# Immediate operands for the exponentials of a fused attention, Fourier and feed-forward kernel, with the scales of q and k chosen to cancel

## The chip, the cores and the metric

The kernel runs on one core of a Trainium2 chip. Its time is the device time of one launch in microseconds, the median of several executions. A core has five engines that run side by side and meet at semaphores: TensorE (PE in the profile, with its weight loads as PEld), VectorE (DVE), ScalarE (ACT), GpSimd (POOL) and SyncE (SP, which issues most DMAs). Each engine takes its own instructions strictly in the order in which the program gives them.

## What is computed

Attention over 8 batches of 8 heads, 576 positions and 64 columns, with a block-causal mask in blocks of 64; then on the joined heads a two-dimensional Fourier transform, whose real part is added, a layer norm and a feed-forward layer. All inputs and outputs are fp32. Cut to what matters here:

```python
scores = (1.0 / np.sqrt(D)) * np.matmul(q, k.transpose(0, 1, 3, 2))      # D = 64: 0.125
scores = np.where(mask, scores, -1000000000.0)
scores = scores - np.max(scores, axis=-1, keepdims=True)
attn = np.exp(scores)
attn = attn / (np.sum(attn, axis=-1, keepdims=True) + 1e-09)
x = np.matmul(attn, v)                                                   # heads joined: (8, 576, 512)
u = x + np.real(np.fft.fft(np.fft.fft(x, axis=1), axis=2))
un = (u - mu) / np.sqrt(var + 1e-06)
out = u + np.maximum(un @ w_ch1, 0.0) @ w_ch2
```

## The kernel before

**Precision by halves.** Matmuls run on pairs of f16 numbers, a high part and the rest, so that three matmuls stand for one in fp32. To split a tensor well, it is first multiplied by a power of two that is worked out on the chip from its sum of squares.

**Heads.** The 64 heads are numbered through. Heads 0 to 7 use q and k as fp32r numbers without such a scale (`lead`, `rest`, lines 421 to 438). Heads 8 to 63 come in pairs g = 4 to 31: `load_pair` brings q and k of two heads, `sum_qk` (line 380) squares them on ACT with a running sum, `scale` (line 461) turns the sums of v, q and k into three powers of two, `high` (line 389) writes the scaled f16 high parts on ACT, `low` (line 396) the rests on DVE, and `high_copies` and `low_copies` send them by DMA into the operands X1 and X0 of the score matmuls.

**scale.** A matmul with ones sums the three columns over the partitions. DVE copies the result to `n2` and works on the bits as integers: the exponent is halved and subtracted from a constant, for all three columns at once (two instructions). Two more instructions, on one column each, hold the scale of q back to a bound and write into column 9 of the tile `vacc` the power of two that undoes both scales and multiplies by 0.125. That column is `exps[g]`.

**One head.** `max_part` (line 576) computes the scores' row maxima in four pieces: matmuls into a PSUM bank, then TENSOR_REDUCE on DVE into the tile `M`. `shift` (line 605) transposes `M` on PE, writes the negative on ACT into `mt`, and a DMA puts it into a row of X1, so that the score matmuls subtract the maximum. `scores` (line 634) makes four pieces per head, two of 288 columns and two of 512: matmuls into a bank, then on ACT the exponential twice, once as f16 (`ph`, line 652) and once as fp32 (`p32`, named `p` in the profile, line 655), then on POOL their difference (`pl`, line 657). `p32` has two buffers, and the bank comes free when both exponentials have read it. `values` (line 663) multiplies by v with the three matmuls per block and on DVE divides by the row sums, which one column of ones in v gives. The exponentials carry a factor of 32 (2 to the PSHIFT), which the division takes out again: heads 0 to 7 get it in the shift row (line 618), heads 8 to 63 as the exponential's bias, a [128, 1] tile `lift` that holds 5 ln 2.

```python
how = {"scale": 0.125} if h < H else {"scale": exps[h // 2], "bias": lift}      # line 637, H = 8
```

**The rest.** `fourier_steps` runs the transform of each batch once its eight heads are done, `normalized_steps` the norm, and `feed_steps` the feed-forward layer, whose matmuls (into `h` and `acc`) are fed to PE between the others. In the first 220 us DVE also unpacks the two weight matrices (`weight_single`, line 1101).

**What sets the order.** The program's order on each engine is written out by a planner that runs when the program is built (lines 286 to 361 and 1205 to 1263). Work comes in steps of a dozen lanes, each with the steps that it follows, a place (about the number of the head) and a chain of costs: "D0.7" is 0.7 us on DVE, A is ACT, G and P POOL, X DVE with the port that it shares with POOL, Q the DMA queue of SP, B marks where a PSUM bank comes free. The planner books these on model queues, picks the next step that is ready, and emits its instructions by their planned start. An exponential of width w is planned with 0.19 + 0.00082 w us on ACT (`_a`, line 51), a `scale` step with 0.11 on PE, 0.2 and, after the bank, 0.7 on DVE (line 569).

Of the kernel before, what the change touches and what calls it, by code (L numbers as in the profile page):

```python
# [9 lines left out]
F32 = mybir.dt.float32  # L10
F32R = mybir.dt.float32r
F16 = mybir.dt.float16
I32 = mybir.dt.int32
AF = mybir.ActivationFunctionType
ALU = mybir.AluOpType
# [4 lines left out]
B, H, S, D = 8, 8, 576, 64  # L20
DM = H * D
FF = 4 * DM
P = 128
# [19 lines left out]
PSHIFT = 5  # L43
# [158 lines left out]
def tile_attn_fourier_ffn(  # L202
# [4 lines left out]
    const = pool("const")  # L207
# [5 lines left out]
    def ps_tile():  # L213
        return ps[current].tile([P, 512], F32, name=current)

    def mm(*args, **kw):
        return tc.keep_in_program_order(nc.tensor.matmul(*args, **kw))  # L217

    def tp(*args, **kw):
        return tc.keep_in_program_order(nc.tensor.transpose(*args, **kw))  # L220

    vector, scalar, gpsimd, sync = (Ordered(tc, x) for x in (nc.vector, nc.scalar, nc.gpsimd, nc.sync))
# [7 lines left out]
    vector.memset(ones, 1.0)  # L230
    mhalf = const.tile([P, 1], F32, name="mhalf")
    vector.memset(mhalf, -0.5)
    lift = const.tile([P, 1], F32, name="lift")
    vector.memset(lift, float(PSHIFT * np.log(2.0)))
    dft = const.tile([P, c_dft.shape[1]], F32R, name="dft")
    o = [0]

# [39 lines left out]
    for at in range(0, NCOS, P):  # L277
        w = min(P, NCOS - at)
# [17 lines left out]
    def may(step):  # L296
        return all(x in done for x in step.after) and all(x in done for x in step.need)

    def ready(step):
        r = max((done[x] for x in step.after), default=0.0)  # L300
        return max(r, min(rings[x][0] for x in lent)) if step.bank else r
# [138 lines left out]
    def load_v(g):  # L440
        V = vraw[g] = work.tile([P, 5, 2, D], F32, name="V", bufs=1)
        sync.dma_start(V.rearrange("p c h d -> p (c h d)"), v[g])
        yield
# [11 lines left out]
    def sum_v(g):  # L455
        acc = sums(g)
        junk = work.tile([P, DM], F32, name="tmp", bufs=2).bitcast(F16)[:, 0:5 * 2 * D]
        scalar.activation(junk, vraw[g].rearrange("p c h d -> p (c h d)"), AF.Square, accum_out=acc[:, 0:1])
        yield

    def scale(g):

        acc = vsums.pop(g)
        t = ps_tile()
        mm(t[:, 0:3], ones, acc[:, 0:3], start=True, stop=True)
        yield
        n2, sc = acc[:, 3:6], acc[:, 6:9]
        x = work.tile([P, 4], I32, name="pw", bufs=2)
        vector.tensor_copy(n2, t[:, 0:3])
        c = 190 + 14  # L470
        vector.tensor_scalar(
            x[:, 0:3], n2.bitcast(I32), 0x7F000000, 1, op0=ALU.bitwise_and, op1=ALU.logical_shift_right
        )
        vector.tensor_scalar(sc.bitcast(I32), x[:, 0:3], -1, c << 23, op0=ALU.mult, op1=ALU.add)
        sq, xk, e = acc[:, 7:8].bitcast(I32), x[:, 2:3], acc[:, 9:10].bitcast(I32)
        vector.scalar_tensor_tensor(sq, xk, (2 * 127 + 20 - c) << 23, sq, op0=ALU.add, op1=ALU.min)
        vector.scalar_tensor_tensor(e, xk, (3 * 127 - 3 - c) << 23, sq, op0=ALU.add, op1=ALU.subtract)
        scales[g] = sc
        exps[g] = acc[:, 9:10]
        yield  # L480

    exps = {}

    def parts_v(g):

        sc = scales[g][:, 0:1]
        V = vraw.pop(g)
        vh, vl = VH[g % 2], VL[g % 2]
        scalar.activation(vh[:, :, :, 0:D], V, AF.Copy, scale=sc)
        yield  # L490
        vector.scalar_tensor_tensor(vl, V, sc, vh[:, :, :, 0:D], op0=ALU.mult, op1=ALU.subtract)
        pairs[g] = sc
        yield

    def split_v(g):

        acc = vsums.pop(g)
        V = vraw.pop(g)
        t = ps_tile()
        mm(t[:, 0:1], ones, acc[:, 0:1], start=True, stop=True)  # L500
        yield
        sc = acc[:, 2:3]
        x = work.tile([P, 1], I32, name="pw", bufs=2)
        vector.tensor_copy(acc[:, 1:2], t[:, 0:1])
        vector.tensor_scalar(
            x, acc[:, 1:2].bitcast(I32), 0x7F000000, 1, op0=ALU.bitwise_and, op1=ALU.logical_shift_right
        )
        vector.tensor_scalar(sc.bitcast(I32), x, -1, (190 + 14) << 23, op0=ALU.mult, op1=ALU.add)
        vh, vl = VH[g % 2], VL[g % 2]
        yield  # L510
        scalar.activation(vh[:, :, :, 0:D], V, AF.Copy, scale=sc)
        yield
        vector.scalar_tensor_tensor(vl, V, sc, vh[:, :, :, 0:D], op0=ALU.mult, op1=ALU.subtract)
        pairs[g] = sc
        yield
# [39 lines left out]
    def v_lane():  # L555
        for g in range(B * H // 2):
            yield Step(
                lambda: load_v(g), 0.0, ("Q0.6", "M1.1", "L2.0"), (("N", g - 1),) if g else (), ("LV", g), place=2 * g - 2.2,
            )
            yield Step(lambda: sum_v(g), 0.0, ("t1", "A0.95", "t"), (("LV", g),) + ((("V", 2 * g - 3, 4),) if 1 < g < H // 2 else (("V", 2 * g - 5, 4),) if g > 3 else ()), ("NS", g),  # L560
                       place=2 * g - (0.6 if g < H // 2 else 1.6))
            if g < H // 2:
                yield Step(
                    lambda: split_v(g), 0.11, ("D0.46", "B", "A0.83", "X0.88"), (("NS", g),), ("N", g), True,
                    need=(("V", 2 * g - 3, 4),) if g > 1 else (), place=2 * g - 0.4,
                )
                continue
            yield Step(
                lambda: scale(g), 0.11, ("D0.2", "B", "D0.7"), (("NS", g), ("QS", g)), ("SC", g), True, place=2 * g - 1.4,
            )  # L570
            yield Step(
                lambda: parts_v(g), 0.0, ("A0.83", "X0.88"), (("SC", g),), ("N", g),
                need=(("V", 2 * g - 3, 4),), place=2 * g - 0.4,
            )
# [30 lines left out]
    def shift(h):  # L605

        t = ps_tile()
        tp(t[0:5, 0:P], M[h % 2][:, 0:5], ident)
        yield
        if h >= H:  # L610
            mt = work.tile([5, P], F32, name="mt", bufs=2).bitcast(F16)[:, 0:P]
            scalar.activation(mt, t[0:5, 0:P], AF.Copy, scale=-(2.0 ** -15))
            yield
            sync.dma_start(X1[h % NB][KM:KS, 0:640].rearrange("r (j p) -> r j p", j=5), mt)
            yield
            return
        mt = work.tile([5, P], F32R, name="mt", bufs=2)
        scalar.activation(mt, t[0:5, 0:P], AF.Copy, bias=float(8.0 * PSHIFT * np.log(2.0)), scale=-1.0)
        yield
        dst = LEAD[h % NB][KM:KS, 0:640].rearrange("r (j p) -> r j p", j=5)  # L620
        sync.dma_start(dst.bitcast(F32), mt.bitcast(F32))
        yield
# [11 lines left out]
    def scores(h, n):  # L634

        x0, x1 = (REST[h % NB], LEAD[h % NB][0:KS]) if h < H else (X0[h % NB], X1[h % NB])
        how = {"scale": 0.125} if h < H else {"scale": exps[h // 2], "bias": lift}
        i, at, chunks = PIECES[n]
        if at == 0:
            width = S if i == 0 else 512  # L640
            probs[h, i] = [work.tile([P, width], F16, name=f"p{x}{i}", bufs=1) for x in "hl"]
        ph, pl = probs[h, i]
        t = ps_tile()
        w = 0
        for c, lo, width in chunks:
            first, last = P * c + lo, P * c + lo + width
            keys = S + (P * c if c < 4 else S - P)
            mm(t[:, w:w + width], x0[:, keys:keys + P], x0[:, first:last], start=(w == 0), stop=False, skip_group_check=True)
            keys, w = keys + 64, w + width
            mm(t[:, w - width:w], x1[:, keys:keys + P], x1[:, 64 + first:64 + last], start=False, stop=True, skip_group_check=True)  # L650
        yield
        scalar.activation(ph[:, at:at + w], t[:, 0:w], AF.Exp, **how)
        yield
        p32 = work.tile([P, 512], F32, name="p32", bufs=2)
        scalar.activation(p32[:, 0:w], t[:, 0:w], AF.Exp, **how)
        yield
        gpsimd.tensor_tensor(pl[:, at:at + w], p32[:, 0:w], ph[:, at:at + w], op=ALU.subtract)
        yield
# [550 lines left out]
    while True:  # L1209
# [13 lines left out]
        for w, side in enumerate(sides):  # L1223
# [3 lines left out]
            at = max(now, ready(side))  # L1227
# [5 lines left out]
        else:  # L1233
            w = None
# [5 lines left out]
        if soon:  # L1240
            i = min(soon, key=lambda i: heads[i].place)
        elif feed and ready(filler) <= now or feed and not able:
            i = None
        elif able:
            i = min(able, key=lambda i: ready(heads[i]))
        elif any(sides):
            w = min((w for w, x in enumerate(sides) if x is not None and may(x)), key=lambda w: ready(sides[w]))
# [62 lines left out]
```

## Time and profile before

| | |
|---|---|
| median of 3 runs | 1267.94 us (1265.29 to 1270.67) |
| the profiled execution | 1268.88 us, its span 1267.1 us |
| TensorE's granted clock, mean | 0.940 |
| busy: PE, PEld, DVE, ACT, POOL | 91%, 66%, 56%, 50%, 35% of the span |

A profile is of one execution. The span runs from the first to the last instruction; an engine's busy time is the time covered by its instructions, and a busy PE is not a PE at its peak. Groups of instructions are told by the engine, the operation and the tiles, written `out<-in`; all instructions here have a helper's line (195, 217 or 220), so the tiles identify them: `ph<-ps,lift,vacc` is the first exponential of a head from 8 on, with its pointers to bias and scale, `ph<-ps` the same of heads 0 to 7. After each group stand the busy time, the mean length of one in ns, and the idle time of the engine before it with what ended that. The chain of work that ended last is followed back from the last instruction, at each step to what released it.

### The profile page before, as it was taken

How to read it: one execution, taken by the hardware profiler on the slowest of the kernel's cores; microseconds unless marked ns; L12 is line 12 of the kernel's file. 1: busy time of each engine (PE TensorE's matmuls, PEld its weight loads, DVE VectorE, ACT ScalarE, POOL GpSimd, SP SyncE). 2: the span in 40 equal slices, each digit the busy share in tenths (PEclk: the TensorE clock that was granted, in tenths of full speed). 3: DMA queues.
4: the chain of work that ended last, by engine and by line, in shares of the span. 5: the costliest groups of instructions: out<-in, count | busy, mean ns of one | idle time of the engine just before them, and what ended most of it. 6: DMA issues, size and time to landing. Idle time of an engine off the chain costs nothing.

```text
span 1267.1 us, 25203 instructions
## 1 busy us (share of the span) xinstructions
PE 1150.4 (91%) x10068; PEld 831.3 (66%) x10068; DVE 711.4 (56%) x1493; ACT 637.3 (50%) x1249; POOL 439.2 (35%) x537
## 2 busy tenths in 40 slices
PE   5772588979899999999999989999999999999998
PEld 4661366557677776677767767677777667766665
DVE  7778797755655575766657555477534424421211
ACT  5556667945666567566656457656652112111110
POOL 5656632433534433444333423425341300300000
PEclk9555787989999999999999989999999999999999
DMA  7675253342224234234233222513320110000000
GB/s 211 195 253 171 71 171 97 97 116 72 84 73 127 62 84 109 73 93 121 63 97 114 72 85 77 154 36 93 73 72 7 36 33 4 22 18 1 18 18 17
DMA packets 64939, 107.34 MB, mean 85 GB/s; under 512 B 9408, under 2 KB 35192, under 8 KB 64822
## 3 DMA queue, kind: packets, MB, share of 16 engines
q1 hardware_dynamic: 57718, 81.42, 23.1%
q10 hardware_dynamic: 4384, 16.78, 3.9%
q0 software_dynamic: 2720, 7.54, 2.1%
q8 instruction: 79, 1.29, 0.4%
q14 instruction: 38, 0.31, 0.1%
HBM read 58.52 MB, written 18.87 MB: 61 GB/s over the span
## 4 chain that ended last, share of the span: by engine, by line
PE 75%; DVE 12%; ACT 4%; DMA 3%; POOL 3%; issue 3%; SPq 0%; DVEq 0%; ACTq 0%; POOLq 0%
PE h L217 27%; PE acc L217 27%; PE ps L217 14%; PE av L217 5%; DVE W L195 3%; DVE M L195 2%; DMA lead<-mt 2%; PE ps L220 1%; ACT ph L195 1%; ACT p L195 1%; DVE tmp L195 1%; POOL pl L195 1%; DVE vacc L195 1%; DVE VL L195 1%; DMA xd<-x 1%
## 5 line engine op out<-in xcount | busy, mean ns | idle before, releaser
L217 PE MATMUL h<-uh,W 128*128 128x256 f16 x2304 | 430.5, 274 | 1.1 <-DVE ul L195 0.6
L195 POOL TENSOR_TENSOR pl<-p,ph 128x512 f16<-128x512 f32 (+1 forms) x256 | 254.6, 1000 | 408.9 <-ACT p L195 382.6
L217 PEld LDWEIGHTS <-W 128*128 128x128 f16 x3456 | 334.3, 98 | 65.9 <-issue 2.8
L217 PE MATMUL acc<-W,gh 128*128 128x512 f16 x1104 | 330.1, 380 | 0.0
L217 PE MATMUL h<-ul,W 128*128 128x256 f16 x1152 | 315.3, 274 | 0.0
L195 ACT ACTIVATE gh<-h 128x512 f16<-128x512 f32 x138 | 82.2, 596 | 269.4 <-PE h L217 269.3
L217 PE MATMUL acc<-W,gl 128*128 128x512 f16 x552 | 209.8, 380 | 0.1
L195 DVE SCALAR_TENSOR_TENSOR gl<-h,gh 128x512 f16<-128x512 f32 x138 | 94.9, 688 | 204.5 <-ACT gh L195 204.2
L195 DVE TENSOR_REDUCE M<-ps 128x1 f32<-128x192 f32 (+3 forms) x289 | 129.9, 486 | 124.4 <-PE ps L217 124.2
L195 ACT ACTIVATE ph<-ps,lift,vacc 128x288 f16<-128x288 f32 x220 | 150.8, 686 | 90.5 <-PE ps L217 90.1
L217 PE MATMUL ps<-lead 72*128 72x64 f16 (+13 forms) x693 | 160.8, 296 | 20.1 <-ACT lead L195 6.7
L217 PEld LDWEIGHTS <-gh 128*128 128x128 f16 x1104 | 104.0, 99 | 81.1 <-issue 2.3
L195 ACT ACTIVATE p<-ps,lift,vacc 128x288 f32<-128x288 f32 x220 | 150.6, 686 | 10.3 <-POOL pl L195 10.3
L217 PEld LDWEIGHTS <-ph 128*128 128x128 f16 x1920 | 115.7, 104 | 27.8 <-issue 4.7
L217 PE MATMUL av<-VH,pl 128*128 128x65 f16 x960 | 117.1, 201 | 17.6 <-POOL pl L195 16.7
L217 PE MATMUL av<-VH,ph 128*128 128x65 f16 x960 | 118.7, 203 | 2.1 <-DVE x L195 2.1
L217 PE MATMUL av<-VL,ph 128*128 128x64 f16 x960 | 118.2, 201 | 0.0
L217 PEld LDWEIGHTS <-pl 128*128 128x128 f16 x960 | 94.3, 103 | 20.6 <-POOL pl L195 19.3
L217 PE MATMUL ps<-rest 128*128 128x288 f16 (+2 forms) x348 | 96.8, 292 | 6.9 <-ACT p L195 2.9
L217 PEld LDWEIGHTS <-gl 128*128 128x128 f16 x552 | 53.9, 98 | 67.1 <-DVE gl L195 1.6
L217 PEld LDWEIGHTS <-lead 72*128 72x128 f16 (+1 forms) x672 | 58.2, 100 | 58.8 <-issue 13.1
L217 PEld LDWEIGHTS <-rest 128*128 128x128 f16 x336 | 33.4, 99 | 19.7 <-issue 2.8
(193 smaller groups left out, 1441.2 us busy)
## 6 DMA issues: line engine op xcount, KB each, us to landing
raw<-in_qk_dram SPq DMA_DIRECT2D x28, 576.0 KB
W<-in_moe_w_ch_dram ACTq DMA_DIRECT2D x14, 1024.0 KB
rest<-lead SPq DMA_DIRECT2D x72, 144.0 KB
V<-in_v_dram SPq DMA_DIRECT2D x32, 320.0 KB
xd<-x SPq DMA_DIRECT2D x32, 256.0 KB
out_dram<-u SPq DMA_DIRECT2D x32, 256.0 KB
rest<-rest SPq DMA_DIRECT2D x56, 144.0 KB
u<-xd SPq DMA_DIRECT2D x8, 512.0 KB
```

The lines of the kernel that those rows point to most:

```text
L195: x = f(*args, **kw)
L217: return tc.keep_in_program_order(nc.tensor.matmul(*args, **kw))
L220: return tc.keep_in_program_order(nc.tensor.transpose(*args, **kw))
```

## The change

It picks the scales of q and k so that their product is one: the exponent of each is a quarter of the exponent of the other's sum of squares minus a quarter of that of its own, both cut to a multiple of four. The scores then need no scale but 0.125, so the exponentials of all heads take the immediate 0.125 and no bias. The factor of 32 goes for all heads into the row that `shift` writes. The scale of v is made as before, in two instructions of its own. `exps`, `lift` and its memset go away. The planner's price for the second part of `scale` on DVE is 0.8 instead of 0.7.

```diff
-    lift = const.tile([P, 1], F32, name="lift")
-    vector.memset(lift, float(PSHIFT * np.log(2.0)))
...
         vector.tensor_copy(n2, t[:, 0:3])
-        c = 190 + 14
+        bits, to = n2.bitcast(I32), sc.bitcast(I32)
         vector.tensor_scalar(
-            x[:, 0:3], n2.bitcast(I32), 0x7F000000, 1, op0=ALU.bitwise_and, op1=ALU.logical_shift_right
+            x[:, 1:3], bits[:, 1:3], 0x7E000000, 2, op0=ALU.bitwise_and, op1=ALU.logical_shift_right
         )
-        vector.tensor_scalar(sc.bitcast(I32), x[:, 0:3], -1, c << 23, op0=ALU.mult, op1=ALU.add)
-        sq, xk, e = acc[:, 7:8].bitcast(I32), x[:, 2:3], acc[:, 9:10].bitcast(I32)
-        vector.scalar_tensor_tensor(sq, xk, (2 * 127 + 20 - c) << 23, sq, op0=ALU.add, op1=ALU.min)
-        vector.scalar_tensor_tensor(e, xk, (3 * 127 - 3 - c) << 23, sq, op0=ALU.add, op1=ALU.subtract)
+        for i in (1, 2):
+            vector.scalar_tensor_tensor(
+                to[:, i:i + 1], x[:, 3 - i:4 - i], 127 << 23, x[:, i:i + 1], op0=ALU.add, op1=ALU.subtract
+            )
+        vector.tensor_scalar(
+            x[:, 0:1], bits[:, 0:1], 0x7F000000, 1, op0=ALU.bitwise_and, op1=ALU.logical_shift_right
+        )
+        vector.tensor_scalar(to[:, 0:1], x[:, 0:1], -1, (190 + 14) << 23, op0=ALU.mult, op1=ALU.add)
         scales[g] = sc
-        exps[g] = acc[:, 9:10]
...
-                lambda: scale(g), 0.11, ("D0.2", "B", "D0.7"), (("NS", g), ("QS", g)), ("SC", g), True, place=2 * g - 1.4,
+                lambda: scale(g), 0.11, ("D0.2", "B", "D0.8"), (("NS", g), ("QS", g)), ("SC", g), True, place=2 * g - 1.4,
...
-            scalar.activation(mt, t[0:5, 0:P], AF.Copy, scale=-(2.0 ** -15))
+            c = 2.0 ** -15
+            scalar.activation(mt, t[0:5, 0:P], AF.Copy, bias=float(8.0 * PSHIFT * np.log(2.0)) * c, scale=-c)
...
-        how = {"scale": 0.125} if h < H else {"scale": exps[h // 2], "bias": lift}
...
-        scalar.activation(ph[:, at:at + w], t[:, 0:w], AF.Exp, **how)
+        scalar.activation(ph[:, at:at + w], t[:, 0:w], AF.Exp, scale=0.125)
...
-        scalar.activation(p32[:, 0:w], t[:, 0:w], AF.Exp, **how)
+        scalar.activation(p32[:, 0:w], t[:, 0:w], AF.Exp, scale=0.125)
```

More of the change, by code (lines that the diff above doesn't have):

```diff
@@ L469, in scale @@
         vector.tensor_copy(n2, t[:, 0:3])
-        c = 190 + 14
+        bits, to = n2.bitcast(I32), sc.bitcast(I32)
         vector.tensor_scalar(
-            x[:, 0:3], n2.bitcast(I32), 0x7F000000, 1, op0=ALU.bitwise_and, op1=ALU.logical_shift_right
+            x[:, 1:3], bits[:, 1:3], 0x7E000000, 2, op0=ALU.bitwise_and, op1=ALU.logical_shift_right
         )
-        vector.tensor_scalar(sc.bitcast(I32), x[:, 0:3], -1, c << 23, op0=ALU.mult, op1=ALU.add)
-        sq, xk, e = acc[:, 7:8].bitcast(I32), x[:, 2:3], acc[:, 9:10].bitcast(I32)
-        vector.scalar_tensor_tensor(sq, xk, (2 * 127 + 20 - c) << 23, sq, op0=ALU.add, op1=ALU.min)
-        vector.scalar_tensor_tensor(e, xk, (3 * 127 - 3 - c) << 23, sq, op0=ALU.add, op1=ALU.subtract)
+        for i in (1, 2):
[6 more added lines that the diff above has]
+        vector.tensor_scalar(to[:, 0:1], x[:, 0:1], -1, (190 + 14) << 23, op0=ALU.mult, op1=ALU.add)
         scales[g] = sc
-        exps[g] = acc[:, 9:10]
         yield
-    exps = {}
     def parts_v(g):
```

## The prediction

> **What bounds the kernel now.** The page comes first: span, engine shares, and the chain of work that ended last.
>
> ```profile
> span 1267.1 us, 25203 instructions
> PE 1150.4 (91%) x10068; PEld 831.3 (66%) x10068; DVE 711.4 (56%) x1493; ACT 637.3 (50%) x1249; POOL 439.2 (35%) x537
> PE 75%; DVE 12%; ACT 4%; DMA 3%; POOL 3%; issue 3%; SPq 0%; DVEq 0%; ACTq 0%; POOLq 0%
> PE h L217 27%; PE acc L217 27%; PE ps L217 14%; PE av L217 5%; DVE W L195 3%; DVE M L195 2%; DMA lead<-mt 2%; PE ps L220 1%; ACT ph L195 1%; ACT p L195 1%; DVE tmp L195 1%; POOL pl L195 1%; DVE vacc L195 1%; DVE VL L195 1%; DMA xd<-x 1%
> ```
>
> PE carries the time. ACT, which the change relieves, is busy for half of the span and holds 4% of the chain. An average over stages says little, so the next view cuts the span into stretches: the exponentials that the change touches (heads 8 and up) lie between 147 and 946 us, as a later table shows. The columns are window, length, then busy time of PE, PEld, DVE, ACT and POOL, the granted clock, the DMA share and GB/s.
>
> ```profile
> 147.00:350.00 203.00, 169.40 (x1594) 121.98 (x1595) 142.55 (x302) 134.76 (x267) 81.41 (x101) 0.89 0.37 104
> 350.00:500.00 150.00, 148.39 (x1444) 107.20 (x1442) 91.36 (x215) 91.77 (x180) 57.43 (x69) 1.00 0.33 88
> 500.00:946.00 446.00, 431.47 (x4219) 313.08 (x4217) 271.17 (x604) 271.61 (x530) 179.79 (x217) 0.99 0.31 86
> 946.00:1267.00 321.00, 316.28 (x2205) 218.14 (x2202) 95.74 (x173) 52.18 (x100) 34.75 (x59) 1.00 0.07 21
> ```
>
> PE idles 203 - 169.4 = 33.6 us in the first stretch, 1.6 in the second, 14.5 in the third: 49.7 us altogether is what any relief of the other engines could win between 147 and 946 us. Whose idle time it is, the waits of PE in that window say (total, times, longest):
>
> ```profile
> PE av L217 <- POOL pl L195: 14.8, 13, 5.9
> PE ps L217 <- ACT p L195: 10.2, 9, 2.4
> PE ps L217 <- DVE M L195: 7.5, 7, 1.6
> PE acc L217 <- DVE M L195: 6.6, 1, 6.6
> ```
>
> The first two are the tail of the exponential path: scores on PE, `ph` and `p` on ACT, `pl` on POOL, values on PE; and a bank of scores comes free when `p` has been read. The last two are row maxima queued on DVE, with no exponential in them.
>
> **The exponentials.** The change turns the two per-partition operands of line 652 and 655 (scale from `vacc`, bias from `lift`) into immediates, for heads 8 to 63. Heads 0 to 7 already run this very call, so the trace holds both forms. First the grouped rows (busy, mean ns), then the window table restricted to the tile `lift` (DVE, then ACT):
>
> ```profile
> L195 ACT ACTIVATE ph<-ps,lift,vacc 128x512 f16<-128x512 f32 x110 | 86.0, 783 | 17.6 <-PE ps L217 17.2
> L195 ACT ACTIVATE ph<-ps,lift,vacc 128x288 f16<-128x288 f32 x110 | 64.9, 590 | 73.0 <-PE ps L217 72.9
> L195 ACT ACTIVATE ph<-ps 128x288 f16<-128x288 f32 x8 | 3.2, 402 | 0.5 <-PE ps L217 0.5
> L195 ACT ACTIVATE ph<-ps 128x512 f16<-128x512 f32 x5 | 3.0, 606 | 1.8 <-PE ps L217 1.8
> 147.00:350.00 203.00, 0.00 (x0) 68.62 (x112) 0.89 0.37 104
> 350.00:946.00 596.00, 0.00 (x0) 204.81 (x336) 0.99 0.32 87
> ```
>
> There are 112 + 336 = 448 such instructions (56 heads, 4 pieces, 2 outputs). One is shorter by 590 - 402 = 188 ns at 288 columns and by 783 - 606 = 177 ns at 512. Neighbours on ACT overlap, though, so the price of one is the distance between starts, read from the timeline:
>
> ```profile
> 604.98 0.58 ACT L195 ACTIVATE p<-ps,lift,vacc 128x288 f32<-128x288 f32 x1
> 605.45 0.59 ACT L195 ACTIVATE ph<-ps,lift,vacc 128x288 f16<-128x288 f32 x1
> 606.40 0.79 ACT L195 ACTIVATE ph<-ps,lift,vacc 128x512 f16<-128x512 f32 x1
> 607.07 0.80 ACT L195 ACTIVATE p<-ps,lift,vacc 128x512 f32<-128x512 f32 x1
> 63.85 0.40 ACT L195 ACTIVATE ph<-ps 128x288 f16<-128x288 f32 x1
> 64.14 0.40 ACT L195 ACTIVATE p<-ps 128x288 f32<-128x288 f32 x1
> 67.14 0.60 ACT L195 ACTIVATE ph<-h 128x512 f16<-128x512 f32 x1
> 67.64 0.59 ACT L195 ACTIVATE p<-h 128x512 f32<-128x512 f32 x1
> ```
>
> With pointers 0.47 and 0.67 us from start to start, with immediates 0.29 and 0.50: the overlap doesn't eat the saving, each instruction gives back 0.17 to 0.18 us, and I take 0.18. ACT gets 448 x 0.18 = 81 us back, but ACT is idle half of the time, so what counts is the part on the path. The chain that ended last, cut to the two stretches, gives that part:
>
> ```profile
> by line: PE h L217 19.7%; PE ps L217 14.0%; PE acc L217 12.5%; DVE W L195 7.6%; DVE M L195 6.1%; PE av L217 5.8%; issue 5.3%; DVE vacc L195 2.5%; ACT p L195 1.9%; POOL pl L195 1.8%; POOL ag L195 1.7%; ACT ph L195 1.6%; POOL u L195 1.5%; PE
> by line: PE acc L217 27.6%; PE h L217 25.7%; PE ps L217 19.8%; PE av L217 8.4%; issue 2.4%; PE ps L220 1.8%; DMA lead<-mt 1.8%; ACT ph L195 1.8%; ACT p L195 1.5%; DVE tmp L195 1.2%; DVE M L195 0.7%; DVE gl L195 0.6%; POOL pl L195 0.6%; DVE
> ```
>
> From 147 to 350 us, `ph` and `p` hold 3.5% of 203 = 7.1 us; from 350 to 946 us 3.3% of 596 = 19.7 us; together 26.8 us. Equal counts of both widths make a mean distance of 0.57 us, of which 0.18 goes, 32%: **-8.5 us**. The bounds: nothing, if PE is late anyway wherever the chain runs through ACT (in the second stretch PE idles only 1.6 us); and all the waits of PE on `p` and `pl`, 10.2 + 14.8, less the single one of 5.9 that ACT doesn't cause: there POOL has its indirect loads in front of `pl`, the last of them the row below. That leaves 19.1 us.
>
> ```profile
> 265.05 0.89 POOL L195 DMA_INDIRECT U<-xd,rows  x1 [0.30 <-issue]
> ```
>
> **The longer scale step.** `scale` issued five DVE instructions per pair of heads (a copy, two on three columns, two on one) and now issues six: the copy, one on two columns, two on one, two more on one for v. That is one more, for 28 pairs. The rows of its present parts:
>
> ```profile
> L195 DVE SCALAR_TENSOR_TENSOR vacc<-pw,vacc 128x1 int32<-128x1 int32 x56 | 14.7, 263 | 1.9
> L195 DVE TENSOR_SCALAR vacc<-pw 128x3 int32<-128x3 int32 x28 | 7.4, 264 | 1.0
> L195 DVE TENSOR_SCALAR pw<-vacc 128x3 int32<-128x3 int32 x28 | 6.6, 236 | 1.0
> ```
>
> One more is 0.25 us, 28 of them 7 us of DVE's time. Queued behind it on DVE stand the next row maxima, whose lateness PE shows above. On the chain `vacc` on DVE holds 2.5% of 203 = 5.1 us; a call puts 2 x 0.263 + 0.264 = 0.79 us there under this name, so some 6.4 calls lie on it, and 6.4 x 0.25 = **+1.6 us**. In 350 to 946 us the name is not among those shown, so it is under 0.6% of 596 = 3.6 us, at most 4.6 calls and 1.1 us. Hence 0 to 2.7 us; I take 1.5, near the row that is there. The scale of q and k is written by the fourth instruction as before, so ACT's `high` copies wait no longer; that of v is now last instead of third, which its step hides, being placed a full head later; without that cover it is two instructions, 0.5 us, in each of those calls.
>
> **Edits with one answer.** The shift now carries the constant as an immediate on a Copy. Both forms are in the trace, without it (f16) and with it (fp32r, heads 0 to 7), and cost the same:
>
> ```profile
> L195 ACT ACTIVATE mt<-ps 5x128 f16<-5x128 f32 x54 | 13.9, 257 | 37.9 <-PE ps L220 37.7
> L195 ACT ACTIVATE mt<-ps 5x128 fp32r<-5x128 f32 x2 | 0.5, 258 | 2.4 <-PE ps L220 2.4
> ```
>
> The memset of `lift` lies at the start beside the first loads: nothing. No DMA, matmul or wait is added or moved in the text; but the planner's price of `scale` on DVE goes from 0.7 to 0.8, which can reorder steps (rival three).
>
> **The clock.** Around 335 us the exponential path holds PE up, and the granted clock falls just after (windows; then PE's waits in 330 to 341 us):
>
> ```profile
> 330.00:340.00 10.00, 5.40 (x61) 3.67 (x59) 7.99 (x18) 8.69 (x17) 5.62 (x8) 1.00 0.36 105
> 340.00:350.00 10.00, 9.55 (x95) 8.31 (x96) 5.58 (x12) 7.61 (x15) 3.30 (x4) 0.83 0.56 159
> PE ps L217 <- ACT p L195: 2.3, 2, 1.3
> PE av L217 <- POOL pl L195: 2.1, 2, 1.1
> PE ps L220 <- DVE M L195: 0.7, 1, 0.7
> ```
>
> A clock of 0.83 over 10 us costs 1.7 us. If those waits shrink far enough the dip goes; I can't tell, and take half, **-0.9 us**. The Trainium skill (TensorE: Matmul & The Clock Gate, HAM oscillation) has it that the clock holds as long as PE has no gap over about 3.4 us; by that rule gaps of 1.3 us cost no clock, and the sum would be -7.0 instead of -7.9. The row speaks against the rule: no wait here is over 1.3 us and the clock went down.
>
> **Sum:** -8.5 + 1.5 - 0.9 = -7.9 us. The profiled execution took 1268.88 us (span 1267.1 and 1.8 around it), 0.9 above the median of 1267.94; taken off the median: **1260.0 us**. A change of 0.5%, 6.3 us, is about what can be told from none.
>
> **Rivals.** *One, PE is the bound and the freed time stays on ACT.* For it: from 350 to 946 us PE is busy 579.9 of 596 us, and three quarters of the chain time counted above lies there. Against it: the waits on `p` and `pl` by name. It gives 0 to -5 us, 1263 to 1268, and up to 1270 with the DVE instruction on the path. A second reading leads there too: measured by weight loads, PE is as full before 946 us as after, 542.3 of 799 us against 218.1 of 321, 68% in both, and after 946 us there are no exponentials to wait for. The Trainium skill (Trainium Kernel Development and Optimization, Performance Expectations) holds load share, not matmul busy time, to be the good measure; by it nothing is to be won and the time stays at 1268. I weigh it low, since the matmuls of the two stretches differ (65-column values matmuls load as often for fewer columns), and the idle gaps are measured directly. Chance 0.21, of it 0.05 for this reading.
>
> *Two, the waits close altogether.* The plan's own prices for an exponential, 0.43 and 0.61 us (line 51's formula), lie below the measured distance now and above it afterwards, so ACT would run to plan; -19.1 + 1.5 - 1.7 = -19.3, 1248.6 us. Against it: where ACT runs without a break, as in 330 to 340 us, six exponentials give 1.1 us where PE waits 4.4. Chance 0.15 for a gain over 12 us.
>
> *Three, the new plan costs more.* Place: the first 220 us, where DVE unpacks the weights while the first paired heads are scaled. The extra 0.1 us in DVE's booked time can put a weight unpacking ahead of a row maximum. Price: PE's one wait of 6.6 us on such a maximum, with a dip of the clock like that above (1.7), 8.3 us. One of them cancels the gain (1268.3); from two on it is slower, 1276.6 us. For it: from 147 to 350 us DVE is the fullest engine but PE, and W on DVE holds 7.6% of the chain. Against: each booking moves by a tenth of a microsecond only, and reordering can as well remove such a wait. Chance 0.09.
>
> That the immediates don't shorten the instruction is ruled out by the rows of heads 0 to 7, and has no chance of its own.
>
> **Numbers.** Forecast (a gain of 5 to 12 us) 0.55, of which 0.12 is under 6.3 us. Faster: 0.43 + 0.15 = 0.58; within 0.5%: 0.12 + 0.21 = 0.33; slower 0.09. The range goes from rival two with no cost on DVE, 1267.9 - 19.1 - 1.7 = 1247, to rival one with the instruction's cost and no gain, 1270; rival three and the edges are left out.
>
> **What would show it.** Right: the exponentials at 402 and 606 ns in all heads, ACT's busy time down by some 80 us, `p` and `pl` waits of PE in 147 to 946 us down by about a third to a half, `ph` and `p` on the chain near 18 us, DVE busy up by 7 us, the stretch after 946 us as long as now. Wrong: durations unchanged; PE's waits moved to row maxima or a DMA with the same total; or new gaps of several microseconds before 220 us.

## The result, and the profile after

The changed kernel takes 1254.01 us (median of 4, 1252.18 to 1254.87) against 1268.18 us before (median of 4): a ratio of 0.9887, 95% interval 0.9863 to 0.9911, or 14.2 us less. The forecast was 1260.0 us, 7.9 less, so the direction and the range held. The experiments below show that its reason did not: nearly all of the gain comes from another order of the same work, and none that could be measured from the shorter exponentials.

The page of the changed kernel, its span, engine shares and chain:

```profile
span 1253.1 us, 25235 instructions
PE 1146.6 (92%) x10068; PEld 829.5 (66%) x10068; DVE 703.6 (56%) x1520; ACT 562.6 (45%) x1249; POOL 441.0 (35%) x537
PE 76%; DVE 11%; DMA 5%; POOL 3%; ACT 2%; issue 2%; SPq 0%; DVEq 0%; POOLq 0%; ACTq 0%
```

ACT's busy time fell from 637.3 to 562.6 us, 75 us, as the change promised. The grouped rows have the new length of the exponentials in all heads, 605 and 412 ns where the pointers took 783 and 590:

```profile
L195 ACT ACTIVATE ph<-ps 128x512 f16<-128x512 f32 x115 | 69.4, 605 | 29.9 <-PE ps L217 29.5
L195 ACT ACTIVATE ph<-ps 128x288 f16<-128x288 f32 x118 | 48.5, 412 | 78.5 <-PE ps L217 78.3
```

The windows in the same stretches as before:

```profile
147.00:350.00 203.00, 173.33 (x1669) 124.66 (x1670) 145.28 (x325) 115.85 (x266) 84.58 (x101) 0.91 0.37 105
350.00:500.00 150.00, 149.93 (x1452) 108.81 (x1449) 88.53 (x202) 79.32 (x184) 61.10 (x72) 1.00 0.32 88
500.00:946.00 446.00, 434.29 (x4210) 315.01 (x4207) 271.37 (x629) 230.69 (x531) 178.89 (x221) 0.99 0.32 89
946.00:1267.00 321.00, 302.98 (x2133) 209.10 (x2130) 90.15 (x165) 48.35 (x92) 30.42 (x52) 1.00 0.06 18
```

From 147 to 946 us PE idles 41.5 us instead of 49.7, and in this one window it does 7322 matmuls instead of 7252. What remains after 946 us, which the prediction had as long as before, is 14.0 us shorter (307.1 us to the end of the span instead of 321.1). PE's waits from 147 to 946 us:

```profile
PE av L217 <- POOL pl L195: 8.4, 5, 6.9
PE acc L217 <- DVE M L195: 6.6, 1, 6.6
PE ps L217 <- ACT p L195: 6.3, 6, 1.9
PE ps L217 <- DVE M L195: 5.7, 5, 1.6
```

The waits on `pl` and `p` fell from 25.0 to 14.7 us, just where the prediction looked and by as much as it asked. Read alone, these rows seem to bear the prediction out, but for the shorter stretch at the end. They can't tell the effect of shorter exponentials from that of another order.

### The profile page after: what moved, and what is told of

The parts are those of the page before. It is cut to its first block, busy times and chain, and to the rows that moved or that the text cites. A ratio compares the mean times of both kernels' runs of the same rounds, so it can differ in the third digit from the quotient of the medians.

```text
span 1253.1 us, 25235 instructions
## 1 busy us (share of the span) xinstructions
PE 1146.6 (92%) x10068; PEld 829.5 (66%) x10068; DVE 703.6 (56%) x1520; ACT 562.6 (45%) x1249; POOL 441.0 (35%) x537
## 4 chain that ended last, share of the span: by engine, by line
PE 76%; DVE 11%; DMA 5%; POOL 3%; ACT 2%; issue 2%; SPq 0%; DVEq 0%; POOLq 0%; ACTq 0%
PE acc L217 28%; PE h L217 27%; PE ps L217 14%; PE av L217 6%; DVE W L195 3%; DVE M L195 2%; PE ps L220 1%; DVE tmp L195 1%; DMA lead<-rest 1%; DMA xd<-x 1%; POOL pl L195 1%; DMA lead<-mt 1%; DVE VL L195 1%; DMA u<-xd,rows 1%; DVE rest L195 1%
## 5 line engine op out<-in xcount | busy, mean ns | idle before, releaser
L195 POOL TENSOR_TENSOR pl<-p,ph 128x288 f16<-128x288 f32 (+1 forms) x256 | 253.3, 1003 | 411.3 <-ACT p L195 384.3
L217 PE MATMUL ps<-lead 73*128 73x288 f16 (+13 forms) x693 | 160.2, 295 | 14.7 <-ACT lead L195 6.8
L195 ACT ACTIVATE ph<-ps 128x512 f16<-128x512 f32 (+1 forms) x233 | 117.9, 507 | 108.4 <-PE ps L217 107.8
L195 ACT ACTIVATE p<-ps 128x512 f32<-128x512 f32 (+1 forms) x233 | 118.1, 508 | 11.5 <-POOL pl L195 11.4
L217 PEld LDWEIGHTS <-lead 73*128 73x128 f16 (+1 forms) x672 | 57.8, 99 | 58.6 <-issue 17.3
```

Source lines behind the costliest of these rows:

```text
L195: x = f(*args, **kw)
```

## The experiments

The change has three parts: the immediates, the sixth DVE instruction of `scale`, and the planner's price 0.8, which makes another order. The lists of instructions show how far the third goes: with the price put back, PE and ACT have exactly the instructions of before in exactly its order (the exponentials apart from their operands); with 0.8 the order of PE departs from it at its 865th matmul, at about 188 us. The expectations below weigh three theories: A, the shorter exponentials do it all; B, they do the 7.9 us of the prediction and the order the rest; C, the order does most of it. So the first four runs cross pointers or immediates with the old or the new order. Ratios below are to the kernel before, from runs on the same chip.

**Immediates in the old order.**

```diff
-                lambda: scale(g), 0.11, ("D0.2", "B", "D0.8"),
+                lambda: scale(g), 0.11, ("D0.2", "B", "D0.7"),
```

> The changed kernel with the planner's price of scale put back from 0.8 to 0.7: immediates and the six-instruction scale step in the order of before (the matmuls and the ACT instructions stand in exactly the order of before). Theory A (the shorter exponentials do it all, the order is neutral): as the changed kernel, 1254 us, within 2 us. Theory B (the prediction's sum of 7.9 us holds for the exponentials and the rest came from the new order): about 1260 us. Theory C (the new order did most of it): 1264 us or more.

Measured: 1266.12 us, ratio 0.9983 (0.9962 to 1.0003). The gain is gone, as theory C had it.

**Before in the new order.** The kernel before with 0.8 in place of 0.7, nothing else.

> The kernel before with only the planner's price of scale raised from 0.7 to 0.8: pointers and the five-instruction scale step in the order of the changed kernel. Theory A: 1268 us, as before, within 2 us. Theory B: about 1262 us. Theory C: 1258 us or less. Rival three of the prediction (a new order can cost): above 1270 us.

Measured: 1255.33 us, ratio 0.9898 (0.9877 to 0.9920). One digit of a planner's price, with the old exponentials, gives 13 us.

**Pointers in the old order,** and **pointers in the new order.** The changed kernel, its exponentials given [128, 1] tiles that hold 0.125 and 0, once with the price 0.7 and once with 0.8:

```diff
+    eighth = const.tile([P, 1], F32, name="eighth")
+    vector.memset(eighth, 0.125)
+    lift = const.tile([P, 1], F32, name="lift")
+    vector.memset(lift, 0.0)
...
+        how = {"scale": 0.125} if h < H else {"scale": eighth, "bias": lift}
...
-        scalar.activation(ph[:, at:at + w], t[:, 0:w], AF.Exp, scale=0.125)
+        scalar.activation(ph[:, at:at + w], t[:, 0:w], AF.Exp, **how)
```

> The changed kernel in the order of before, with the exponentials of heads 8 to 63 given their scale and bias through [128, 1] tiles again (constants 0.125 and 0): the same result, the six-instruction scale step, the old length of the exponentials. Against before it prices the sixth DVE instruction alone: the prediction has +1.5 us (0 to 2.7), so 1268 to 1271 us; if the sixth instruction is free, 1268 us. Against the run of the immediates in the old order it prices the pointers alone: theory A has 14 us or more, theory B 8 to 9 us, theory C under 4 us.

> The changed kernel with only the pointers put back (constant tiles for 0.125 and 0), in its own new order. Against the changed kernel it prices the pointers in the new order. Theory A: 1268 us, so the whole difference is the pointers'. Theory B: 1262 to 1264 us. Theory C: 1258 us or less. If pointers and order only add up, the distance to the changed kernel equals that between the two runs in the old order within 2 us; if the new order suits the shorter exponentials, it is larger here.

Measured: 1264.90 us in the old order, ratio 0.9986 (0.9966 to 1.0005), and 1254.28 us in the new one, 0.9890 (0.9869 to 0.9911). The four together:

| | old order (0.7) | new order (0.8) |
|---|---|---|
| before: pointers, five instructions | 1 | 0.9898 |
| pointers, six instructions | 0.9986 | 0.9890 |
| immediates, six instructions | 0.9983 | 0.9887 (the change) |

Down a column little changes, across a row one per cent. Theory C stands, A and B fall. By these ratios the pointers are worth 0.03% in either order; in the old one, with twelve executions of each, the means are 1265.6 and 1265.5 us, standard deviation 3 us, so their difference is 0.1 us give or take 2.5. The sixth instruction has no cost that could be measured: 0.9986 is 1.8 us below before, the interval from 4.3 below to 0.6 above.

Where the 75 us off ACT went is looked for in PE's waits first (147 to 946 us). First pointers in the old order, then immediates in the old order, then pointers in the new order:

```profile
PE av L217 <- POOL pl L195: 12.6, 11, 6.0
PE ps L217 <- ACT p L195: 9.6, 9, 2.1
```

```profile
PE av L217 <- POOL pl L195: 14.1, 11, 6.4
PE ps L217 <- ACT p L195: 8.2, 10, 1.7
```

```profile
PE av L217 <- POOL pl L195: 7.9, 6, 5.6
PE ps L217 <- ACT p L195: 5.1, 6, 1.3
```

22.2 us, 22.3 us, 13.0 us: the waits go with the order, not with the exponentials. Shorter ones take 1.4 us off the waits on `p` and add 1.5 us to those on `pl`. These are single profiles, and such small differences are within their scatter: before, with pointers in the old order too, had 25.0 us. One place where time is lost on `pl` can be watched at some 390 us, where both kernels have the same instructions. Before, POOL's and ACT's timeline:

```profile
392.85 0.89 POOL L195 DMA_INDIRECT U<-xd,rows  x1 [0.30 <-issue]
395.01 0.52 POOL L195 MEMSET u<- 1x512 f32 x1 [1.27 <-DMA u<-xd,rows]
396.18 1.42 POOL L195 TENSOR_TENSOR pl<-p,ph 128x288 f16<-128x288 f32 x2
390.38 0.59 ACT L195 ACTIVATE ph<-ps,lift,vacc 128x288 f16<-128x288 f32 x1 [1.71 <-PE ps L217]
396.94 1.47 ACT L195 ACTIVATE p<-ps,lift,vacc 128x512 f32<-128x512 f32 x2 [2.89 <-POOL pl L195]
```

and with immediates in the old order:

```profile
388.66 0.89 POOL L195 DMA_INDIRECT U<-xd,rows  x1 [0.30 <-issue]
392.77 0.51 POOL L195 MEMSET u<- 1x512 f32 x1 [3.22 <-DMA u<-xd,rows]
393.94 1.41 POOL L195 TENSOR_TENSOR pl<-p,ph 128x288 f16<-128x288 f32 x2
386.64 0.41 ACT L195 ACTIVATE ph<-ps 128x288 f16<-128x288 f32 x1 [1.85 <-PE ps L217]
394.70 1.28 ACT L195 ACTIVATE p<-ps 128x512 f32<-128x512 f32 x2 [4.58 <-POOL pl L195]
```

ACT begins this head 3.7 us earlier, but POOL has the three indirect loads of a Fourier stage in front of `pl`, stands 3.22 us instead of 1.27 until they have landed, and takes `pl` up only 2.2 us earlier. ACT's third `p` needs a buffer of `p32` that only `pl` frees, so ACT stands for 4.58 us instead of 2.89. What ACT gained here, it waits for POOL, and POOL for a DMA. How long that takes differs between executions: the mixture of two orders timed further down has the same instructions at this place, and in its profile POOL stood 0.88 us for the loads and ACT 2.25 us for `pl`. So this head shows a path on which ACT's gain can be lost, and not how much of it is lost on average. The chain that ended last points the same way for the whole run, by one per cent (page of the immediates in the old order; before, ACT had 4% and POOL 3%):

```profile
PE 73%; DVE 13%; POOL 4%; issue 3%; ACT 3%; DMA 3%; SPq 0%; DVEq 0%; POOLq 0%; ACTq 0%
```

To test this, POOL was taken off the path. Theory P in the expectations has PE late anyway, whatever POOL does; theory Q has POOL next in line behind ACT.

**Without `pl`, pointers, and without `pl`, immediates,** both in the old order. The low part of the attention is left out; all exponentials and all matmuls stay.

```diff
-                (ph, vh[:, c, hh], D + 1), (ph, vl[:, c, hh], D), (pl, vh[:, c, hh], D + 1)
+                (ph, vh[:, c, hh], D + 1), (ph, vl[:, c, hh], D), (ph, vh[:, c, hh], D + 1)
...
-        gpsimd.tensor_tensor(pl[:, at:at + w], p32[:, 0:w], ph[:, at:at + w], op=ALU.subtract)
```

> The pointers in the old order, without POOL's subtraction that makes pl: POOL's instruction is left out and the third values matmul reads ph in its place, so PE has the same matmuls, the exponentials are all still made, and the attention loses its low part. Base for the next run. Theory P (PE is late anyway, POOL doesn't matter): 1262 to 1266 us, with PE's waits on pl, some 14 us, taken over by others. Theory Q (POOL is the next in line behind ACT): the waits on pl go, 1252 to 1258 us.

> The immediates in the old order without POOL's subtraction, as in the run before it (the low part of the attention left out). With POOL out of the path the shorter exponentials meet PE directly. Theory Q (the freed time of ACT was lost on POOL): 5 to 9 us below the run with pointers and without pl. Theory P (the path through ACT had slack all along): within 2 us of it.

Measured: 1241.46 us with pointers, ratio 0.9800 (0.9771 to 0.9829), and 1234.89 us with immediates, 0.9766 (0.9740 to 0.9792). POOL's subtraction costs 1.9%, 24 us, more than theory Q said, though POOL is busy for only 35% of the span. And now the immediates are worth something: the means of six executions each are 1240.2 and 1235.1 us, a difference of 5.1, give or take 3.7. That is at the lower edge of theory Q's 5 to 9 us, and its interval, 1.4 to 8.8, only just reaches into theory P's 2 us; against the 0.1 us with `pl` it is 5.0 us more, give or take 4.3. So theory Q is the better supported, by a narrow margin and with one reserve. Taking POOL's work away doesn't only shorten the path, it also speeds up DVE. The engine shares and the weight unpacking, pointers with `pl` and then without:

```profile
PE 1150.4 (91%) x10068; PEld 830.8 (66%) x10068; DVE 706.2 (56%) x1522; ACT 636.4 (50%) x1249; POOL 439.6 (35%) x537
L195 DVE SCALAR_TENSOR_TENSOR W<-W 128x1024 int32<-128x1024 int32 x28 | 41.6, 1486 | 0.8
```

```profile
PE 1140.3 (92%) x10068; PEld 823.6 (66%) x10068; DVE 673.9 (54%) x1522; ACT 634.5 (51%) x1249; POOL 185.9 (15%) x281
L195 DVE SCALAR_TENSOR_TENSOR W<-W 128x1024 int32<-128x1024 int32 x28 | 37.6, 1343 | 0.8
```

The same 1522 DVE instructions take 32 us less. Of the 26.6 us between these two profiled spans (1266.6 and 1240.0 us), 12.1 are there by PE's 865th matmul (187.5 and 175.4 us), while DVE still unpacks weights. How much of the 24 us is the path and how much a faster DVE, the runs don't separate; the two runs without `pl` share the faster DVE, so their 5 us don't come from it.

**More work for ACT.** Pointers in the old order, and a copy of one column behind each of the 448 exponentials:

```diff
         scalar.activation(ph[:, at:at + w], t[:, 0:w], AF.Exp, **how)
+        if h >= H:
+            scalar.copy(spare, ones[:, 0:1])
...
```

> The pointers in the old order with one more tiny ACT instruction (a copy of one column, about 0.16 to 0.2 us from start to start) behind each of the 448 exponentials of heads 8 to 63: 72 to 90 us more for ACT, as much as the immediates took away. If the path through ACT has slack on both sides (theory P), 1265 to 1269 us. If the kernel stands at the point where ACT begins to bind, so that less costs nothing and more does, 1272 to 1285 us. If every exponential on the chain counts, as the prediction had it, 8 to 9 us more than the pointers alone.

Measured: 1271.79 us, ratio 1.0051 (1.0028 to 1.0074), which is 0.65% or 8.2 us (give or take 3.8) over the pointers alone. The dose was smaller than planned: ACT's busy time rose by 38 us only, since the copies overlap with their neighbours.

```profile
PE 1153.2 (91%) x10068; PEld 831.8 (66%) x10068; DVE 705.6 (56%) x1522; ACT 674.4 (53%) x1697; POOL 440.2 (35%) x537
L195 ACT COPY spare<-ones 128x1 f32<-128x1 f32 x448 | 86.8, 194 | 0.0
```

So 38 us more for ACT cost some 8 us, and 74 us less (636.4 to 562.4) bring none that can be measured. The 8.2 us are also what the third expectation had, by the prediction's way of reckoning, but for 72 to 90 us of copies; for copies of 0.085 us that way gives 26.8 x 0.085 / 0.57 = 4.0. One slope doesn't fit both sides: with pointers the kernel stands at a kink. That ACT and POOL are late together there, so that lengthening ACT shows at once and shortening it uncovers POOL, fits the two runs without `pl`; no run shows it directly.

**What the order is worth.** That leaves the 13 us of the new order. Four further prices of `scale` and of the exponentials, all with immediates and six instructions, show what a redrawn plan does. Theory L says that any price draws another order, whose time lies anywhere in a band of some 1%; theory D, that a dearer and so truer price makes a better plan.

> The changed kernel with the planner's price of scale at 0.9 instead of 0.8: a third order. Theory L (any other price draws another order, whose time lies anywhere in a band of some 1%, and 0.7 was a poor draw or 0.8 a good one): anywhere from 1250 to 1270 us. Theory D (a dearer and so truer price of scale makes a better plan): at or below 1254 us.

> The changed kernel with the planner's price of scale at 0.6, below the old 0.7: a fourth order. Theory L (any price draws another order, and the old 0.7 was a poor draw): anywhere in 1250 to 1266 us, more likely near the 1254 and 1255 us of 0.8 and 0.9 than near the 1266 us of 0.7. Theory D (a dearer price makes a better plan): 1266 us or more.

> The changed kernel with the planner's price of scale at 1.0. Theory D: at or below 1254 us. Theory L: anywhere in 1250 to 1266 us.

```diff
+def _e(width):
+    return f"A{0.05 + 0.00084 * width}"
...
-                    lambda n=n: scores(h, n), w / 1200.0, (_a(w), "p1", _a(w), "B", _g(w), "p"),
+                    lambda n=n: scores(h, n), w / 1200.0, (_e(w), "p1", _e(w), "B", _g(w), "p"),
```

> The changed kernel with the planner's price of one exponential put to the measured distance of two with immediates: 0.29 us at 288 columns and 0.48 us at 512, in place of 0.43 and 0.61. If the plan gains from knowing what ACT now takes, 1245 to 1251 us, below the changed kernel. If the freed time of ACT is worth nothing while POOL makes pl, it is one more order: anywhere in 1250 to 1266 us. Rival: a plan that counts on ACT without slack leaves PE waiting more, above 1260 us.

and 0.8 for pairs from 16 on, 0.7 below:

> The changed kernel with the planner's price of scale at 0.7 for pairs below 16 and 0.8 from there on, so that the order is the old one for about the first half of the heads. If the old order loses its time early (the weights' stage and the first feed-forward tiles, before some 470 us), 1264 us or more; if it loses it late (the waits near 530, 680 and 745 us), 1254 to 1258 us; if it loses a little in many places, about 1260 us.

| price of `scale` | us | ratio to before, interval |
|---|---|---|
| 0.6 | 1250.85 | 0.9859 (0.9833 to 0.9885) |
| 0.7 | 1266.12 | 0.9983 (0.9962 to 1.0003) |
| 0.8, the change | 1254.01 | 0.9887 (0.9863 to 0.9911) |
| 0.9 | 1255.09 | 0.9923 (0.9900 to 0.9947) |
| 1.0 | 1261.45 | 0.9939 (0.9916 to 0.9963) |
| 0.7 below pair 16, 0.8 above | 1248.28 | 0.9845 (0.9818 to 0.9872) |
| 0.8, exponentials at 0.29 and 0.48 | 1258.36 | 0.9922 (0.9898 to 0.9946) |

Theory D falls: the dearest price is among the slowest, the cheapest among the fastest. A plan that knows ACT's true time is no better either. Seven orders of the same work lie in a band of 1.4%, without a trend in the price, and the order of before is the slowest of the seven. The largest gain comes from a mixture that nobody would choose for a reason, and lies below everything that was expected of it. Its ratio is 0.4% below that of the changed kernel, but the two intervals overlap a little. TensorE's mean granted clock does not tell the orders apart: the kernel before in the new order took 1256.63 us in the execution with a mean clock of 0.980, and 1255.10 in one with 0.943.

That mixture also shows where the old order loses in its second half. It is the old order until PE's two lists part at their 4260th matmul, which starts at 565.6 us with immediates in the old order and at 560.5 us in the mixture. These 5.1 us came about with the same instructions in the same order, so they belong to the execution and not to the order; the other 13.8 us between the two spans (1264.4 and 1245.5 us) come after. From 560 to 946 us, immediates in the old order and then the mixture, PE's window row and its waits on `p` and `pl` (the mixture has none on `p`):

```profile
560.00:946.00 386.00, 374.13 (x3712) 271.24 (x3710) 232.28 (x536) 198.91 (x457) 154.61 (x180) 1.00 0.31 87
PE ps L217 <- ACT p L195: 3.6, 4, 1.7
PE av L217 <- POOL pl L195: 1.6, 1, 1.6
```

```profile
147.00:560.00 413.00, 379.79 (x3640) 275.50 (x3641) 277.01 (x628) 225.76 (x520) 171.97 (x208) 0.95 0.35 98
560.00:946.00 386.00, 383.20 (x3770) 278.45 (x3769) 234.65 (x544) 201.74 (x467) 154.19 (x184) 1.00 0.33 88
PE av L217 <- POOL pl L195: 1.3, 1, 1.3
```

PE idles 2.8 us there instead of 11.9. No single wait accounts for it: several of one to three microseconds, on `p`, on row maxima, on the DMA of `mt`, are gone where other matmuls stand in the queue at that moment. The new order of the change gains in more places: with pointers in both, PE's idle time falls from 32.4 to 29.3 us between 147 and 350 us, from 1.5 to 0.0 up to 500 us, and from 15.3 to 10.2 us up to 946 us. PE fills that time with feed-forward matmuls: behind the last exponential 1272 of them into `h` are left instead of 1344, and 657 into `acc` instead of 672, with the pointers as they were (before, against before in the new order). Which reordered step pays in it stays open, and whether part of `pl` could move from POOL to DVE was not tried.

## Why the prediction came out right, and where its working was wrong

*Length of the exponentials:* right. 605 and 412 ns against 606 and 402 forecast, and 75 us off ACT against 81. The Trainium skill (ScalarE: Activation LUTs, What ACT_TABLE_LOAD costs) gives about 93 ns for each [128, 1] operand; the rows agree, 178 ns for two of them at both widths.

*"-8.5 us" for the exponentials on the chain:* wrong, and this is the step that failed. Measured 0.1 us give or take 2.5 in the old order, 0.03% in the new one. The shares of `ph` and `p` on the chain were read rightly, but the chain is one path, and the step multiplied its length by the saving as if no other path were within 8 us of it. With the order held, PE's waits on `p` fell by 1.4 us only and those on `pl` did not fall. The runs point to POOL's path as the next one, with the same heads and the same two buffers of `p32`: without `pl` the same immediates are worth 5.1 us, give or take 3.7. Asking what is late next when `p` comes earlier would have led to `pl`, whose waits the prediction counted in its bound. The outcome for this part is that of rival one, and its reason, PE bound anyway, isn't the whole of it, since PE still waits 22 us on this path.

*"+1.5 us" for the sixth instruction:* too high; -1.8 us, from -4.3 to +0.6. The step did not get longer: the rows of its integer instructions (`pw` and `vacc`) add up to 28.3 us with pointers and six instructions against 29.9 us before, since an added TENSOR_SCALAR on one column takes some 0.15 us and not 0.25. DVE's busy time in the changed kernel fell by 8 us instead of rising by 7.

*"-0.9 us" for the clock:* nothing to be seen. With immediates in the old order PE's waits on `p` and `pl` around 330 us shrank from 4.4 to 3.0 us, but the dip stayed: the granted clock was 0.85 from 330 to 340 us and 0.98 in the 10 us after, where before it was 1.00 and 0.83.

*The planner's price:* rival three had the place of the effect, a redrawn order, and the wrong sign. It set a price for one bad draw and named the good one only in passing; its chance of 0.09 was for the loss. Measured by itself the redraw gives 1.0%, between 0.8 and 1.2%. That the forecast of -7.9 us had the right sign, and about half the size of the -14.2 measured, is therefore chance.

*What was to show it:* the prediction listed `p` and `pl` waits down by a third to a half as a sign of its mechanism. They are down by 41%, for another reason: with pointers the new order has 13.0 us. A sign that two causes share tells nothing between them. Another sign did speak, against the mechanism: the stretch behind the heads was to stay as long as now. With immediates in the old order it does, and the heads end earlier: the last exponential ends at 939.5 us instead of 943.4, with 324.9 us behind it instead of 323.7. In the changed kernel the heads end hardly earlier, at 941.7 us, and what shrinks is the stretch behind them, to 311.4 us, as it does with pointers in the new order (311.0 us).

*Load share as a measure:* the second reading of rival one, by which nothing was to be won before 946 us since it was as full as the stretch after, did not hold. The mixture fits 275.5 + 278.45 = 554.0 us of weight loads into 147 to 946 us, 69% instead of 68%, and is 1.5% faster. PE's idle time there moved more visibly, from 49.7 to 36.0 us.

## What to carry to other kernels

Before a saving on an engine is multiplied by its share of the chain, look at the next engine on the same path and at the buffers between them. Here 74 us off one engine brought nothing that could be measured, and 38 us more on it cost 8. Where a planner or scheduler orders the program, a change of any cost in it is a change of order, and must be timed by itself: the same edit with the old order, and the old kernel with the new one. If orders scatter by more than the effects that are hunted, time several draws before an edit gets the credit or the blame.

## What the runs showed of the hardware that was not expected

POOL's subtractions cost DVE time: without the 256 of them, the same 1522 DVE instructions took 673.9 instead of 706.2 us, and one of the weights' integer instructions 1343 instead of 1486 ns. A one-column ACT copy, 194 ns long in the profile, adds only some 85 ns of busy time (38 us for 448) when it stands behind an exponential.
